# Rewriting an attention-plus-gate kernel as a stream of pair steps, with one PSUM rotation and the weights loaded behind batch 0

## The chip, the cores and the metric

The kernel runs on one core of one Trainium2 chip. The metric is device microseconds (us) of one execution, as the median of several runs. "PE" is TensorE, "DVE" VectorE, "ACT" ScalarE, "POOL" GpSimd. The granted clock is the share of full speed that the profile shows for PE; matmuls at full clock are called warm, those at half clock cold.

## The reference

Two stages follow each other for each of 8 batches (8 heads, 576 rows, 64 columns a head, 128 random features). The first is a random-feature attention; its output, laid out as 576 x 512, goes into a gated convolution that the kernel's authors and this text call "hyena".

```python
def phi(x):
    proj = np.einsum('bhsd,md->bhsm', x, omega)
    return np.concatenate([np.cos(proj), np.sin(proj)], axis=-1) / np.sqrt(m)
q_p, k_p = phi(q), phi(k)
kv  = np.einsum('bhsm,bhsd->bhmd', k_p, v);   z   = np.sum(k_p, axis=2)
num = np.einsum('bhsm,bhmd->bhsd', q_p, kv);  den = np.einsum('bhsm,bhm->bhs', q_p, z)
x = (num / den)                                # [...] guard of den, layout to (8, 576, 512)

proj = x @ w_proj;  x1, x2, x3 = proj[..., :D], proj[..., D:2*D], proj[..., 2*D:]
x2_conv = np.fft.irfft(np.fft.rfft(x2, axis=1) * np.fft.rfft(filter_fft, axis=0), axis=1)
out = (x1 * x2_conv * x3) @ w_out
```

## The kernel before

Heads go two at a time ("a pair"). A pair's features take a fixed path: a matmul with omega (`thk`, `thq`), DVE turns the phase into integer turns, POOL adds a quarter turn for the cosine (both write `angk`, `angq`), ACT takes the sine (`kf`, `qf`). `kv` and `nd` are the products with v and with q, `kvz` and `xsd` what DVE makes of them, `tx` a transpose into `xT`. In hyena, `eo` folds `xT` into even and odd halves, `x2p` projects it, `yp` and `ym` go to the spectrum, DVE multiplies by the filter (`tc`, `ymix`), POOL adds (`yg`), `xc` goes back, the gates (`x3p`, `x1p`) multiply, and `op` projects the output. The code is shortened.

```python
pt = tile_pool(name="pt", bufs=1, space=PSUM)     # phases, 2 banks
ph = tile_pool(name="ph", bufs=3, space=PSUM)     # attention
pm = tile_pool(name="pm", bufs=3, space=PSUM)     # filter and hyena
# [...] weights, filter and its spectrum first, then:
for b0 in range(B + 1):
    # [...] loads of q, k, v of batch b0; all v casts; all q transposes; tail features
    for hp in range(4):                           # attention of batch b0
        # k features of pair hp, q features of pair hp, each through _phases
        kvp = ph.tile([128, 2, 2, 1 + D], FP32, tag="ph")    # 40 matmuls on kf, kft
        nc.vector.tensor_scalar(kvz, kvp, 1.0 / KVS, None, ALU.mult)
        # nd, reciprocal, xsd ; the transpose of pair hp-1 stands between k and q features
    # then hyena of batch b0 - 1, all its PSUM tiles from pm
    eo = mo.tile([128, 4, 2, HS], FP16, tag="eo")
    # [...] x2p, yp, ym, four times (gates, inverse), op

def _phases(nc, pool, th, name):
    turns = pool.tile([128, 2, w], I32, tag="ang")
    nc.vector.tensor_scalar(turns[:, 0], th, TO_PHASE, None, ALU.mult)
    nc.gpsimd.tensor_scalar(turns[:, 1], turns[:, 0], 1.0, TURN / 4, ALU.mult, ALU.add)
    # [...] low 16 bits go to the sine
```

## Time and profile before

| | |
|---|---|
| time before the change | 531.08 us, 3 runs (530.04 to 532.85) |
| profiled span | 532.2 us |
| attention of batch 0, alone | about 50 us, at half clock |
| steady period (attention of b with hyena of b-1) | 54 to 58 us |
| hyena of the last batch, alone | 42 us |

Two rows of the page: the first is the granted TensorE clock in 40 equal slices of the span, in tenths (9 is 90% or more); the second shares out the chain of work that ended last, by engine.

```profile
PEclk9985565689998999999998999899999999999898
...
POOL 25%; DVE 19%; PE 18%; ACT 18%; issue 11%; DMA 6%; SPq 1%; POOLq 0%; DVEq 0%; ACTq 0%
```

The clock is low for long around batch 0's attention only. From 98.8 to 490 us, where the matmuls of both stages lie side by side, its mean is 0.98. No engine has more than a quarter of the chain: the steady stage is a relay from engine to engine, and PE has work of the other stage while it waits.

### The profile page before, as it was taken

The numbers are of one execution on the slowest core, as the hardware profiler recorded it, in microseconds if no ns is written. First come the engines' busy times: TensorE is split into PE (matmuls) and PEld (weight loads), VectorE is DVE, ScalarE is ACT, GpSimd is POOL, SyncE is SP. The second block draws the span as 40 slices with busy tenths as digits, with TensorE's granted clock in tenths as the row PEclk, the third lists the DMA queues.
The fourth block names the chain that finished last, engine by engine and source line by source line (L and its number), as shares of the span: only waits on it lengthen the run. The fifth ranks groups of instructions, "written<-read, shape, count | busy, mean of one in ns | idle before, by whom it ended". The sixth has DMA issues, their size and how long they took to land.

```text
span 532.2 us, 9767 instructions
## 1 busy us (share of the span) xinstructions
PE 390.3 (73%) x4042; PEld 250.4 (47%) x4042; DVE 307.1 (58%) x610; ACT 238.3 (45%) x316; POOL 249.7 (47%) x229
## 2 busy tenths in 40 slices
PE   0135456877897789768877888778967897778794
PEld 0012345445654555446535664456545654564371
DVE  1256435566754766567746684667567665763440
ACT  1012354245635463835563644466355635463222
POOL 3053943546446463655465456455246423442331
PEclk9985565689998999999998999899999999999898
DMA  8859943900366034901590058203400020002002
GB/s 247 232 122 144 108 33 40 139 1 1 46 174 51 1 41 127 102 1 12 119 140 2 1 103 153 16 1 46 164 10 1 3 80 10 1 2 77 14 0 89
DMA packets 71355, 35.30 MB, mean 66 GB/s; under 512 B 47760, under 2 KB 64656, under 8 KB 71312
## 3 DMA queue, kind: packets, MB, share of 16 engines
q0 software_dynamic: 51472, 11.56, 24.1%
q1 hardware_dynamic: 19840, 23.14, 13.4%
q8 instruction: 31, 0.51, 0.4%
q14 instruction: 12, 0.10, 0.1%
HBM read 36.80 MB, written 9.44 MB: 87 GB/s over the span
## 4 chain that ended last, share of the span: by engine, by line
POOL 25%; DVE 19%; PE 18%; ACT 18%; issue 11%; DMA 6%; SPq 1%; POOLq 0%; DVEq 0%; ACTq 0%
ACT qf L317 8%; POOL yT L415 6%; DVE angk L457 5%; POOL yg L383 5%; ACT kf L305 4%; DMA f<-in_moe_filter_fft_dram 4%; POOL angq L458 4%; DVE tc L380 4%; PE kv L331 3%; POOL qa L228 3%; POOL angk L458 3%; PE nd L341 3%; DVE xsd L350 3%; PE xc L94 2%; PE op L94 2%
## 5 line engine op out<-in xcount | busy, mean ns | idle before, releaser
L305 ACT ACTIVATE kf<-angk 128x2048 f16<-128x2048 int16 x32 | 61.1, 1908 | 48.6 <-POOL angk L458 48.6
L317 ACT ACTIVATE qf<-angq 128x2048 f16<-128x2048 int16 x32 | 61.1, 1911 | 21.3 <-POOL angq L458 21.3
L238 POOL TENSOR_TENSOR vl<-vf,vh 128x512 f16<-128x512 f32 x32 | 36.1, 1138 | 72.1 <-PE nd L341 43.1
L94 PEld LDWEIGHTS <-wph 128*128 128x128 f16 x512 | 48.7, 99 | 38.7 <-issue 24.7
L331 PEld LDWEIGHTS <-kf 128*128 128x128 f16 x1024 | 46.2, 105 | 43.5 <-ACT kf L305 43.5
L415 POOL TENSOR_TENSOR yT<-w,cv 128x576 f16<-128x576 f32 x32 | 45.4, 1417 | 40.1 <-DVE cv L414 35.5
L331 PE MATMUL kv<-vh,kf 128*128 128x65 f16 x512 | 40.7, 206 | 30.1 <-ACT kf L305 30.1
L458 POOL TENSOR_SCALAR angk<-angk 128x1024 int32<-128x1024 int32 x32 | 33.6, 1051 | 52.7 <-DVE angk L457 52.2
L397 ACT ACTIVATE x<-x3p 128x288 f32<-128x288 f32 x64 | 26.1, 409 | 69.6 <-PE x3p L94 68.6
L94 PE MATMUL x3p<-xT,wph 128*128 128x288 f16 x256 | 43.8, 290 | 15.8 <-DVE tc L380 11.8
L457 DVE TENSOR_SCALAR angq<-thq 128x1024 int32<-128x1024 f32 x32 | 39.1, 1222 | 19.3 <-ACT qf L282 11.5
L383 POOL TENSOR_TENSOR yg<-tc,tc 128x1024 f16<-128x1024 f32 x16 | 37.6, 2352 | 23.0 <-DVE tc L380 23.0
L228 POOL DMA_DIRECT2D qa<-in_q_dram x40 | 34.8, 887 | 22.4 <-PE tkt L259 13.1
L457 DVE TENSOR_SCALAR angk<-thk 128x1024 int32<-128x1024 f32 x32 | 39.1, 1221 | 10.4 <-PE thk L299 10.2
L94 PE MATMUL op<-wo,yT 128*128 128x512 f16 (+1 forms) x160 | 41.2, 380 | 4.8 <-POOL yT L415 4.1
L94 PE MATMUL x1p<-xT,wph 128*128 128x288 f16 x256 | 41.1, 290 | 3.9 <-DVE tc L380 1.8
L94 PE MATMUL x2p<-wph,eo 128*128 128x512 f16 x160 | 40.2, 386 | 3.2 <-ACT o L429 3.0
L429 ACT ACTIVATE o<-op 128x512 f32<-128x512 f32 (+1 forms) x40 | 23.0, 595 | 43.3 <-PE op L94 28.2
L94 PE MATMUL xc<-invh,yg 128*128 128x288 f16 x128 | 35.2, 289 | 8.7 <-DVE w L403 7.5
L458 POOL TENSOR_SCALAR angq<-angq 128x1024 int32<-128x1024 int32 x32 | 33.5, 1047 | 13.1 <-DVE angq L457 9.8
L341 PE MATMUL nd<-kvz,qf 128*128 128x65 f16 x640 | 27.5, 200 | 16.4 <-ACT qf L317 13.8
L331 PE MATMUL kv<-vl,kf 128*128 128x64 f16 x512 | 39.5, 204 | 0.0
(91 smaller groups left out, 822.4 us busy)
## 6 DMA issues: line engine op xcount, KB each, us to landing
vf<-in_v_dram SPq DMA_DIRECT2D x8, 1024.0 KB, 5.7
out_dram<-o SPq DMA_DIRECT2D x32, 256.0 KB, 2.2
ka<-in_k_dram POOLq DMA_DIRECT2D x8, 512.0 KB, 6.1
qa<-in_q_dram POOLq DMA_DIRECT2D x32, 128.0 KB, 4.2
f<-in_moe_filter_fft_dram SPq DMA_DIRECT2D x8, 256.0 KB, 12.5
wph<-in_moe_w_proj_dram POOLq DMA_DIRECT2D x4, 384.0 KB, 11.4
vft<-in_v_dram SPq DMA_DIRECT2D x16, 64.0 KB, 4.2
out_dram<-o SPq DMA_DIRECT2D x8, 128.0 KB, 2.7
```

The costliest lines, as they stand in the source:

```text
L94: nc.tensor.matmul(outap, l, r, start=(i == 0), stop=(i == n - 1))
L228: nc.gpsimd.dma_start(qall[: CH[c], c], q[b, :, 128 * c : 128 * c + CH[c], :].rearrange("h s d -> s h d"),)
L238: nc.gpsimd.tensor_tensor(vl[hp], vp, vh[hp][:, :, :, :D], ALU.subtract)
L305: nc.scalar.activation(kf.rearrange("p t a r m -> p t (a r m)"), ang, AF.Sin, scale=TO_ANGLE)
L317: nc.scalar.activation(qf[hp][:, :, :, :512].rearrange("p h t s -> p t h s"), ang.rearrange("p t (h s) -> p t h s", h=2), AF.Sin, scale=TO ...
L331: nc.tensor.matmul(kvp[:, hh, t, : 1 + D] if i < 5 else kvp[:, hh, t, :D], l, r_, start=(i == 0), stop=(i == len(terms) - 1),)
L341: nc.tensor.matmul(xps[:, c], qf[hp][:, hh, t, SOFF[c] : SOFF[c] + 128], kvz[:, hh, t], start=(t == 0), stop=(t == 1),)
L383: nc.gpsimd.tensor_tensor(yg[g], t[0], t[1], ALU.add)
L397: nc.scalar.mul(x3[:, ns], ps, YS / TIS)
L415: nc.gpsimd.tensor_tensor(yT[:, dc], w.rearrange("p a s -> p (a s)"), cv.rearrange("p a s -> p (a s)"), ALU.mult)
L457: nc.vector.tensor_scalar(turns[:, 0], th, TO_PHASE, None, ALU.mult)
L458: nc.gpsimd.tensor_scalar(turns[:, 1], turns[:, 0], 1.0, TURN / 4, ALU.mult, ALU.add)
```

## The change

The intent: features of the next pair are emitted ahead of this pair's products, so that PE need not wait for phase, quarter turn and sine of its own pair. The q features go in wider groups, some copies vanish, the weights and the filter are emitted behind the loads of batch 0, and all PSUM tiles but the phases share one rotation of six banks (one pool whose buffers are handed out in turn). It is a complete rewrite; this is its core.

```diff
-    pt = tile_pool(name="pt", bufs=1, PSUM)
-    ph = tile_pool(name="ph", bufs=3, PSUM)
-    pm = tile_pool(name="pm", bufs=3, PSUM)
+        self.pt = self.pool("pt", 1, space=psum)
+        self.ps = self.pool("ps", 6, space=psum)      # every tile has tag "ps"
 [...]
-    # weights, filter, spectrum; then per batch:
-    #   loads(b), v casts(b), q transposes(b), tails(b)
-    #   for hp: features(b, hp); products(b, hp)
-    #   hyena(b - 1)
+        self.omega_load()
+        self.loads(0)
+        self.buffers()
+        self.weights()                                # with the filter's spectrum
+        for b in range(B):
+            if b + 1 < B:
+                self.loads(b + 1)
+            if b == 0:
+                for hp in range(4):
+                    self.v_split(0, hp)
+                self.front(0, 0)
+            for hp in range(4):
+                if hp < 3:
+                    self.front(b, hp + 1)             # features of the next pair
+                elif b + 1 < B:
+                    self.front(b + 1, 0)
+                self.kv(b, hp)
+                if b + 1 < B:
+                    self.v_split(b + 1, hp)
+                self.attend(b, hp)
+                if hp:
+                    self.strip(b, hp - 1)
+            self.strip(b, 3)
+            if b:
+                self.hyena(b - 1)
+        self.hyena(B - 1)
 [...]
-            nc.scalar.mul(x3[:, ns], ps, YS / TIS)    # gates: x3, then w = x1p * x3
+                    nc.scalar.mul(w[:, ns], ps, YS / TIS)
+                    nc.vector.tensor_tensor(w[:, ns], ps, w[:, ns], ALU.mult)
-    t = mo.tile([128, 2, DM], FP32, tag=f"tc{i}")
+    t = mo.tile([128, 2, DM], FP32, tag=f"tc{i}", bufs=2)
```

## The prediction

> **What bounds the kernel now.** I read the page first (busy shares), then stretches of the run by stage, then the chain of work that ended last, then single engines in time.
>
> ```profile
> PE 390.3 (73%) x4042; PEld 250.4 (47%) x4042; DVE 307.1 (58%) x610; ACT 238.3 (45%) x316; POOL 249.7 (47%) x229
> ```
>
> No engine is full, so the answer lies in the stages. The columns of the next view are start:end, length, then busy us (instructions) of PE, PEld, DVE, ACT, POOL, then the granted clock, DMA share and GB/s.
>
> ```profile
> 0.00:24.81 24.81, 0.54 (x2) 0.34 (x3) 2.93 (x12) 1.80 (x3) 5.21 (x13) 1.00 0.95 257
> 48.60:98.80 50.20, 29.68 (x327) 22.16 (x327) 24.49 (x51) 19.71 (x17) 27.80 (x30) 0.53 0.71 87
> 213.00:270.00 57.00, 45.86 (x518) 29.65 (x518) 36.73 (x75) 29.96 (x40) 31.15 (x29) 1.00 0.41 68
> 490.00:532.20 42.20, 30.69 (x169) 17.42 (x168) 12.26 (x21) 11.82 (x25) 10.32 (x6) 0.87 0.13 44
> ```
>
> Four stages: a start in which only DMA works; batch 0, whose attention runs alone at half clock (50 us); seven steady periods of 54 to 58 us (mean 56, from 98.8 to 490) in which attention of batch b runs between the matmuls of the gate stage ("hyena") of batch b-1; and the last hyena alone (42 us). One attention alone plus one hyena alone is 50+42 = 92 us; together they take 56. That overlap is the kernel's main asset. The chain inside a steady period shows why it isn't shorter:
>
> ```profile
> 241.30 1.23 DVE angk L457
> 242.53 0.08 issue
> 242.60 1.04 POOL angk L458
> 243.65 1.38 POOL yT L415
> 245.02 1.02 POOL angq L458
> 246.04 0.02 issue
> 246.07 1.92 ACT qf L317
> 247.99 0.05 issue
> 248.03 0.50 PE nd L341 x10
> ```
>
> The start-to-start distance of a pair is 9.2 us (angk at 241.30, then at 250.46): DVE phase, POOL quarter turn, ACT sine, PE product, one after the other, with hyena work filling PE's gaps.
>
> **What the Trainium skill says.** (1) "TensorE: Matmul & The Clock Gate", Part 1: the default clock is half rate, a window of about 3.4 us decides, and its table of advice warns of idle gaps over about 3 us. The trace agrees on half rate but shows that less idling is enough. PE idled 2.44 us and the next matmuls ran at 0.50 for some 6 us:
>
> ```profile
> 501.49 1.12 PE L94 MATMUL x3p<-xT,wph 128*128 128x288 f16 x4 [2.44 <-DVE tc L380]
> 502.00:503.00 1.00, 0.60 (x3) 0.21 (x2) 1.00 (x2) 0.36 (x1) 0.36 (x1) 0.50 0.00 0
> 506.00:507.00 1.00, 1.00 (x6) 0.65 (x5) 0.46 (x1) 0.00 (x0) 0.00 (x0) 0.50 0.00 0
> ```
>
> (2) The same page, "Architectural detail": PE pulls weight loads ahead, but matmuls stay in program order, and ACT and DVE are strict FIFO. So the compiled order of each engine decides what can overlap. (3) "Trainium Kernel Development and Optimization", Key Constraints: DMAs of all queues run on the same 16 engines. The start agrees: both queues together filled them (share 0.95).
>
> **The change part by part.** I compared the compiled order of both kernels, engine by engine.
>
> *Lost overlap.* Before, PE's order alternates: kv of pair 1, xc, nd, x3p, x1p, kv of pair 2. After, in batches 2 to 7 it is all of the attention, then all of hyena (x2p, yp, ym, four times gates and inverse, op), then the next attention; DVE, ACT and POOL likewise. The separate three-bank PSUM pools became one rotation of six banks, handed out in emission order; I take that as the likely reason. So a steady period becomes A + H instead of about max(A, H).
>
> *H, from the rows of the lone hyena at the end of before.* There, x2p starts at 490.23 and op ends at 525.33: 35.1 us. The new kernel double-buffers tc and has six banks. tc costs 4 x 1.15 us start to start; the second yg (2.35) follows the fourth tc. With x2p 4.35, the first yp 0.65: 5.0+4.7+2.4 is about 12.3 us to the first inverse matmul, against 15.7 before. Then 1.5 for the first inverse, 3 x 3.63 for the other column blocks (before shows 3.6), 2.4 for od, cv and yT, 3.1 for op: 30.2 us. If the clock is low at its start, as I expect, about 2 us more: **H = 32**.
>
> *A, from the same rows.* DVE per batch: eight phases 9.2, two half phases 1.1, copies kT, qT, kTt 3.1, kvz 1.4, reciprocals and xsd 4.8, xT 1.5, v tails 1.6, eo 1.5: 24.2 us. That is the floor. POOL: 7 whole and 2 half turns and 4 vl (13.5) plus its DMA issues (0.89 x5, 0.64 x2, 0.95: 6.7) = 20 us. ACT: 8 sines of 1.91, two of 1.06, four casts of 0.61 = 19.8. PE 16. Walking the compiled orders from op's end: kf of pair 1 waits behind three qa issues (2.7 us) on POOL, so kv_1 at 6.6; kf_2 waits for qf_1_0, a cast and qf_1_1 on ACT, so kv_2 at 14.3; thk_3 stands inside kv_2 in PE's order, so kf_3 needs DVE, POOL and ACT after it: kv_3 at 19.4; its nd waits for the angle of the next batch's pair 0, 23.4; then rd, xsd, one more phase, two xT copies and eo (5.6 us of DVE) before x2p can start: 29.9. Looking one pair ahead is thus partly undone inside PE's fixed order. PE stands nearly still for 5 us at the end of A, enough by the 2.44 us case to lose the clock. With 1.5 us for slow matmuls: **A = 31.5**.
>
> *Start.* Batch 0's q, k and v now go first. But DVE's order has all five folds of the filter before kTt, ACT's order has ten filter copies before the first sine, so features still wait for the filter.
>
> ```profile
> q0 software_dynamic: 51472, 11.56, 24.1%
> q1 hardware_dynamic: 19840, 23.14, 13.4%
> ```
>
> The hardware queue moves 23.14 MB in 13.4% of 532 us (71 us): 325 GB/s. Up to the filter it now has v 1.18, fwd 0.98, filter 2.36 MB: 14 us. The software queue's q and k cost (128-11)/8 = 15 us a batch (11 us being the weights at the start, a share of 43.6% over 25 us), and share the engines. So the filter lands at about 30 us; kv_0 follows 9 us later (filter copies 5, table load 1.3, two sines 3): 38 us as the start of A0 on A's clock. A0 runs at half clock but without eo: 31 us.
>
> *Smaller.* Two-gate product in place, one xT copy fewer a pair, wider tail sines: 16 ACT and 38 DVE instructions fewer, under 1 us a batch.
>
> *Sum.* Start 38, A0 31, A1 31.5; hyenas 0 to 6, 7 x 32 = 224; A2 to A5 126; A6 without loads 29; A7 without a successor 24; the last hyena 29 as its head overlaps the one before; output 6: 538.5. Against before: start and batch 0, 98.8 becomes 69 (-30); end -8; seven periods of 56 become six of some 63 plus the first of 31.5 and one extra hyena in a row (+45).
>
> **The rivals.** (a) *The pipeline wins.* If the waits in A are shorter than I walked (A = 27, near DVE's 24.2) and the clock holds (H = 30), the seven A and seven H lose some 45 us: 495 to 505. For it: PE is busier per us than in batch 0 of before, and before's steady stage held a clock of 0.95 to 1.00. Against: the strict orders, POOL's DMA issues in front of angk, and 5 us of nearly idle PE at each seam. (b) *The clock falls in every A and stays low into H.* Batch 0 before shows 0.53 throughout. A = 34 and H = 34 make 560 to 570. Against: PE's hyena is dense, so recovery after 4 to 6 us is likely. (c) *DMA becomes the wait:* the single vf buffer is reloaded only after the last vl. A vf load takes 5.7 us to land and has a whole H to do it, so it is hidden; no change. (d) *The filter lands earlier or later* than 30 us: one for one, perhaps 5 us.
>
> **Range and chances.** A and H each have an error of about 2 us, common to six or seven repetitions, so 12 to 18 us; the start 5 to 7. I choose **538 us**, range 510 to 564. Faster by 2% means below 520.5, slower above 541.7. The centre is close to the upper border, and a rewrite with fewer instructions has upside I may have missed: faster 0.23, same 0.37, slower 0.40.
>
> **What would show each step.** The stretches of a steady period should show two alternating parts: one with PE near 16 busy us in about 31, DVE nearly full; one with PE near full for 30 to 33 and DVE, ACT, POOL each under half. PEclk should dip once a period, at the start of x2p. Summed DVE busy should drop little (about 10 us), PE's hardly. The first kv should start near 39 us, the second batch near 69. The first xc of a block should come 12 to 14 us after its x2p. I am wrong if hyena and attention overlap after all (a period under 58 us), if A is DVE-full without waits (about 26), or if the first kv starts before 33 us.

## The result, and the profile after

The changed kernel takes 557.59 us (4 runs, 555.85 to 562.23) against 531.97 us of the kernel before (4 runs in the same rounds, 530.04 to 534.3). The ratio is 1.0493, 95% interval 1.0412 to 1.0575: slower. A ratio here is the mean time of one kernel's fast runs over the mean of the other's fast runs of the same rounds, so it isn't quite the ratio of the medians. The profiled execution has a span of 560.4 us, and a mean granted clock of 0.85 against 0.919 before.

From the page of the changed kernel: busy time, clock by slice, and the chain by engine.

```profile
PE 413.3 (74%) x3994; PEld 275.1 (49%) x3994; DVE 309.0 (55%) x580; ACT 247.6 (44%) x300; POOL 252.4 (45%) x237
...
PEclk9865779888967897788968899778987789898998
...
PE 37%; POOL 21%; DVE 21%; DMA 7%; ACT 7%; issue 6%; POOLq 0%; DVEq 0%; ACTq 0%
```

PE executes 48 matmuls fewer and is busy 23 us longer, because the clock is now low in parts of every period. Its share of the chain has doubled.

The stages, cut at each start of `x2p` and each end of `op` (columns as in the prediction; the first stretch is cut at 44 us instead): the first four pairs and batch 1's attention, one attention and one hyena of the steady part, and the last hyena.

```profile
44.00:110.60 66.60, 43.73 (x645) 33.31 (x645) 50.39 (x94) 43.16 (x32) 45.21 (x49) 0.78 0.62 89
...
210.12:241.59 31.47, 21.38 (x329) 17.10 (x330) 24.36 (x46) 19.43 (x16) 20.48 (x22) 0.78 0.70 106
241.59:274.90 33.31, 29.68 (x171) 17.32 (x169) 13.77 (x24) 10.70 (x20) 10.50 (x7) 0.90 0.03 12
...
523.97:560.40 36.43, 26.59 (x169) 16.18 (x169) 11.98 (x21) 12.05 (x25) 10.28 (x6) 0.94 0.16 55
```

Attention (31.47 us) and hyena (33.31 us) stand one after the other; the place where they meet is called the seam below. In attention DVE has 24.36 us of 31.47, in hyena only 13.77; PE nearly fills hyena. One steady period is 64.8 us. The compiled order of PE shows why. Each word is a group of matmuls by tile, pair and count, around the first `x2p` of each kernel, first before, then after:

```
before: x2p_4x4 kv_0x40 yp_0_0x3 yp_0_1x3 nd_0_0x10 nd_0_1x10 tk_1x4 yp_1_0x3 yp_1_1x3 [...]
        x1p_0_0x4 x1p_0_1x4 kv_1x40 xc_0_0x6 xc_0_1x3 nd_1_0x10 nd_1_1x10 [...]
after:  kv_2x24 nd_2_0x10 nd_2_1x10 tx_1x5 tktx2 tk_0x4 tq_0x5 tq_1x5 kv_3x14 thtx4 kv_3x26 thk_0x4
        nd_3_0x10 nd_3_1x10 tx_2x5 thq_0_0x2 thq_0_1x2 tx_3x5 x2p_0x4 x2p_1x4 x2p_2x4 x2p_3x4 [...]
```

The head of one steady hyena in the chain that ended last (start us, us, what):

```profile
241.59 6.02 PE x2p L94 x20
...
249.06 2.28 DVE tc L432 x2
...
251.41 4.66 POOL yg L433 x2
...
256.11 3.06 PE xc L94 x12
```

Warm `x2p` takes 4.33 us and a warm `xc` group of 12 takes 1.47 us (the later groups of the same hyena do). Here the `xc` group is at half clock throughout and `x2p` for the most part. The waits of PE in front of such places (start, us, instruction, and in brackets the idle time before it and who ended it):

```profile
235.80 1.01 PE L342 MATMUL thq<-qT,om 128*128 128x512 f16 x2 [2.67 <-DVE angk L301]
...
256.11 0.42 PE L94 MATMUL xc<-invh,yg 128*128 128x288 f16 x1 [2.89 <-POOL yg L433]
```

And the start: DVE's part of the first tail phases (`angt`), POOL up to their quarter turn, and the first `kv` on PE:

```profile
28.82 0.69 DVE L301 TENSOR_SCALAR angt<-tht 128x512 int32<-128x512 f32 x1 [1.36 <-PE tht L311]
...
34.29 4.19 POOL L227 DMA_DIRECT2D qa<-in_q_dram  x5 [0.92 <-DMA wp<-in_moe_w_proj_dram]
38.55 4.37 POOL L290 TENSOR_TENSOR vl<-vf,vh 128x512 f16<-128x512 f32 x4
42.86 0.64 POOL L302 TENSOR_SCALAR angt<-angt 128x512 int32<-128x512 int32 x1
...
46.71 0.43 PE L372 MATMUL kv<-vh,kf 128*128 128x65 f16 x4
```

DVE had finished its part of `angt` at 29.5 us. POOL first issues five q loads of batch 1, then splits v, and gets to the quarter turn 13.4 us later. The first `kv` starts at 46.7 us.

Where the 22 us between the predicted 538.5 and the profiled 560.4 us lie:

| stage | predicted us | profiled us |
|---|---|---|
| start to the first `kv` | 38 | 46.7 |
| first `kv` to the first `x2p` (two attentions) | 62.5 | 63.9 |
| seven hyenas (0 to 6) | 224 | 233.9 |
| attention of batches 2 to 5 | 126 | 126.1 |
| attention of batches 6 and 7 | 53 | 53.3 |
| last hyena and output | 35 | 36.4 |

### The profile page after: what moved, and what is told of

It is laid out like the page before. It is cut to its first block, busy times and chain, and to the rows that moved or that the text cites. A ratio compares the mean times of both kernels' runs of the same rounds, so it can differ in the third digit from the quotient of the medians.

```text
span 560.4 us, 9625 instructions
## 1 busy us (share of the span) xinstructions
PE 413.3 (74%) x3994; PEld 275.1 (49%) x3994; DVE 309.0 (55%) x580; ACT 247.6 (44%) x300; POOL 252.4 (45%) x237
## 4 chain that ended last, share of the span: by engine, by line
PE 37%; POOL 21%; DVE 21%; DMA 7%; ACT 7%; issue 6%; POOLq 0%; DVEq 0%; ACTq 0%
PE xc L94 9%; PE x2p L94 8%; PE xg L94 7%; POOL yg L433 7%; ACT kf L329 4%; PE kv L372 4%; DVE angq L301 4%; POOL qa L227 4%; DVE tc L432 3%; PE op L94 3%; POOL yT L470 3%; POOL angk L302 3%; DMA qa<-in_q_dram 3%; DVE angk L301 3%; POOL vl L290 3%
## 5 line engine op out<-in xcount | busy, mean ns | idle before, releaser
L94 PE MATMUL xg<-xT,wp 128*128 128x288 f16 x512 | 69.2, 289 | 0.0
L94 PEld LDWEIGHTS <-wp 128*128 128x128 f16 x512 | 51.1, 100 | 15.6
L301 DVE TENSOR_SCALAR angq<-thq 128x1024 int32<-128x1024 f32 (+1 forms) x40 | 44.5, 1112 | 22.1 <-ACT kft L316 11.5
L342 PE MATMUL thq<-qT,om 128*128 128x512 f16 x64 | 23.3, 452 | 39.1 <-DVE angq L301 22.6
L302 POOL TENSOR_SCALAR angq<-angq 128x1024 int32<-128x1024 int32 (+1 forms) x40 | 40.2, 1006 | 25.5 <-DVE angq L301 24.4
L449 ACT ACTIVATE w<-xg 128x288 f32<-128x288 f32 x64 | 26.3, 411 | 56.3 <-PE xg L94 54.9
L94 PE MATMUL x2p<-wp,eo 128*128 128x512 f16 x160 | 47.9, 470 | 0.0
L468 DVE TENSOR_TENSOR cv<-xc,od 128x288 f32<-128x288 f32 x32 | 14.6, 458 | 58.3 <-PE xc L94 58.3
L466 ACT COPY od<-xc 128x288 f32<-128x288 f32 x32 | 12.8, 400 | 71.3 <-PE xc L94 71.3
L389 PEld LDWEIGHTS <-qf 128*128 128x128 f16 x640 | 31.2, 111 | 25.7 <-issue 19.7
```

Source lines behind the costliest of these rows:

```text
L94: nc.tensor.matmul(outap, l, r, start=(i == 0), stop=(i == n - 1))
L301: self.nc.vector.tensor_scalar(t[:, 0], th, TO_PHASE, None, ALU.mult)
L302: self.nc.gpsimd.tensor_scalar(t[:, 1], t[:, 0], 1.0, TURN / 4, ALU.mult, ALU.add)
L342: nc.tensor.matmul(th[:, 512 * i : 512 * (i + 1)], self.om2[:, hh], qT[:, 1024 * g + 512 * i : 1024 * g + 512 * (i + 1)], start=True, stop ...
L389: nc.tensor.matmul(ps[:, c], qf[:, t, hh, o : o + 128], kvz[:, hh, t], start=(t == 0), stop=(t == 1))
L449: nc.scalar.mul(w[:, ns], ps, YS / TIS)
```

## The experiments

The theory after the comparison had four parts. (1) One PSUM rotation in emission order makes attention and hyena serial, and this is the loss. (2) Looking one pair ahead is a gain, which the loss outweighs. (3) Hyena is longer than worked out because the clock falls at the seam, with `eo` as a second suspect. (4) The start is long because POOL's queue is in the way, not because of the filter. The rivals: that the new emission order itself (front of the next pair first) does the serializing; that lookahead is worthless; that `eo` and not the clock is the excess of hyena; and that the filter is what the features wait for. Ten kernels were run; all gave correct results. Kernels that differ from the changed kernel are compared with it by way of the kernel before, which ran in the same rounds.

### 1. The kernel before, with one rotation of six banks

```diff
-    ph = tile_pool(name="ph", bufs=3, PSUM)
-    pm = tile_pool(name="pm", bufs=3, PSUM)
+    ph = pm = tile_pool(name="ps", bufs=6, PSUM)     # and every tag "ph", "pm" becomes "ps"
```

> The kernel before with its two three-bank PSUM pools made one rotation of six, nothing else. Theory (the shared rotation in emission order takes the overlap of attention and hyena away): the compiled order is serial, a period becomes about 43 us of attention plus 32 of hyena, the whole 620 to 660 us. Rival (the overlap was lost for another reason, the rewrite's emission order, and six banks in one pool harm nothing): within 3% of 532.

Measured: 725.68 us, ratio 1.3628 (1.3534 to 1.3722). The direction was right, the size too small in my expectation. The clock row of its page:

```profile
PEclk9955555589766986578755796668955797559998
```

A period is 82 to 85 us. In the steady attentions the mean clock is 0.56 to 0.66, so that `kv` is slow as well. Nothing but the pools was changed, and the overlap is gone: with this emission order the rotation alone is enough to lose it. My explanation: a tile in a shared rotation waits for the tile handed out six before it, and with all of attention emitted ahead of all of hyena, hyena's first tile comes behind attention's last. The Trainium skill, "Perfetto Trace Analysis", section "Matmul Optimizations", asks to use all 8 PSUM banks for parallelism. Both kernels use all 8; what differs is which stages share a rotation, and this run shows 36% for it.

### 2. The changed kernel, with two rotations of three banks again

```diff
-        self.ps = self.pool("ps", 6, space=psum)
+        self.ps = self.pool("ps", 3, space=psum)
+        self.pg = self.pool("pg", 3, space=psum)     # hyena and the filter's spectrum take pg
```

> The changed kernel with the six-bank pool split into three for attention and three for hyena and filter. Theory (lost overlap costs the time): x2p, yp and ym move between the next pairs' products, the period falls from 64.7 to 52 to 58 us, the whole to 490 to 525 us. Rival (the clock and the chain inside attention cost the time, not the seams between the stages): the period stays above 62, the whole within 2% of 557.

Measured: 495.89 us, ratio 0.9324 (0.9276 to 0.9372): 7% faster than the kernel before, where the changed kernel is 5% slower. Its steady periods are 53 to 57 us. The compiled order of PE has both stages mixed again:

```
thk_1x4 kv_0x40 thq_1_0x2 x2p_0x4 x2p_1x2 thq_1_1x2 nd_0_0x10 nd_0_1x10 tk_2x4 x2p_1x2 x2p_2x4 x2p_3x1 kv_1x11 thk_2x4 kv_1x29 x2p_3x3 nd_1_0x10 [...]
```

Its page:

```profile
PE 382.1 (78%) x3994; PEld 249.9 (51%) x3994; DVE 312.5 (64%) x580; ACT 242.7 (49%) x300; POOL 253.7 (52%) x237
```

The same 3994 matmuls now take 382.1 us of PE, not 413.3, at a mean clock of 0.94. So the serial order costs the changed kernel twice, by waiting and by the clock. The emission order of the rewrite is unchanged here, so it doesn't serialize the stages by itself: the rival falls.

### 3. The changed kernel without the lookahead

```diff
-                if hp < 3:
-                    self.front(b, hp + 1)
-                elif b + 1 < B:
-                    self.front(b + 1, 0)
+                self.front(b, hp)                    # and no front(0, 0) ahead of the loop
```

> The changed kernel with each pair's features emitted in the pair's own step again, the rest as it is (serial stages, six banks in one rotation). Theory (looking one pair ahead shortens attention, the intended gain is real): attention grows from 31.5 to 42 to 52 us, as in the merged form of the kernel before; the hyena block stays at 33; the whole 640 to 720 us. Rival (PE's fixed order had undone the lookahead): attention stays under 36, the whole under 600.

Measured: 682.8 us, ratio 1.2804 (1.2748 to 1.286). The chain of this kernel, at the end of one hyena and the start of the next:

```profile
249.56 2.88 PE op L94 x12
...
301.04 4.33 PE x2p L94 x20
```

Attention lies between 252.4 and 301.0 us: 48.6 us, where the changed kernel needs 31.5. The lookahead is therefore worth some 17 us a batch in the serial form. (The mean clock of attention is lower as well, 0.65 against 0.78, so a part of this may be the clock.) The change contains a large gain and a larger loss.

### 4. The changed kernel with PE kept busy at the seam

```diff
+    def warm(self, name, n):
+        ps = self.bank([128, DM], name)
+        for _ in range(n):
+            self.nc.tensor.matmul(ps, self.ident, self.wp[0][:, :DM], start=True, stop=True)
 [...]  # 4 and 5 of them at the end of attention, 9 ahead of the first inverse; nothing reads them
```

> The changed kernel with matmuls that nothing reads put into PE's idle stretches: 4 and 5 at the seam before hyena, 9 ahead of the first inverse of each hyena. Clock theory: x2p falls from 6.0 to about 4.4 us and the first inverse pair from 3.06 to about 1.5, so 3 us in each of 8 hyenas, 20 to 25 us in all (532 to 540). Rival (the low clock lies beside other waits and costs nothing): within 1% of 557, or slower by the matmuls added.

Measured: 542.22 us, ratio 1.0175 (1.0126 to 1.0224), a little above what was expected. 144 matmuls that nobody reads make the kernel faster by (1.0493 - 1.0175) x 532 = 17 us. From the chain of one hyena of it:

```profile
233.37 4.33 PE x2p L94 x20
...
246.22 1.65 PE xc L94 x12
```

`x2p` is at 4.33 us in every hyena, and the first `xc` group takes 1.65 us instead of 3.06. The low clock in hyena is a cost of its own, and it comes from the thin PE work at the seam. This isn't offered as a cure; experiment 2 fills the same gaps with useful work.

### 5. The changed kernel with batch 1's loads, the weights and the filter behind batch 0's first pairs

```diff
         self.buffers()
-        self.weights()
 [...]  # in the pair loop of batch 0:
+                    if hp == 0:
+                        self.loads(1)
+                    elif hp == 1:
+                        self.weights()
+                    elif hp == 3:
+                        for i in range(4):
+                            self.v_split(1, i)
```

> The changed kernel with batch 1's loads issued after pair 0 of batch 0 and the weights after pair 1. Theory (POOL, stuck in its own queue behind the issues of weights and of batch 1's loads until 42.9 us, holds the first features): the first kv comes at 25 to 31 us and not at 46.7, the first hyena at 92 to 100 and not at 110.6, the whole 10 to 18 us shorter. Rival (the filter or q's landing at 26.7 us holds it): the first kv stays after 38 us, the gain is under 6 us.

Measured: 541.01 us, ratio 1.0144 (1.0089 to 1.0198). One of the four runs, at 547.43 us, counts as slow; the ratio is from the other three (538.4 to 541.55). POOL now gets to the quarter turn at 12.67 us and the first `kv` starts at 29.46:

```profile
12.67 0.61 POOL L302 TENSOR_SCALAR angt<-angt 128x512 int32<-128x512 int32 x1 [4.33 <-DVE angt L301]
...
29.46 0.42 PE L372 MATMUL kv<-vh,kf 128*128 128x65 f16 x4
```

The first `x2p` moves from 110.59 to 94.95 us; the next three periods stay at 64.7 to 65.4 us. A start that does the two things at once doesn't tell POOL's queue from the filter, so the next run moves one of them.

### 6. The changed kernel with only batch 1's loads moved

```diff
-            if b + 1 < B:
-                self.loads(b + 1)
             if b == 0:
                 for hp in range(4):
                     self.v_split(0, hp)
                 self.front(0, 0)
+            if b + 1 < B:
+                self.loads(b + 1)
```

> The changed kernel with one move: batch 1's q, k and v loads are issued after batch 0's v casts and the features of its first pair, not before them; the weights stay where they are. Theory (POOL's queue held up the start): POOL is then free for the first vl and the quarter turn once the wo issues are out, at some 27 us, so the first kv moves from 46.7 us to 34 to 36, all later stages shift by 8 to 12 us, and the ratio to the kernel before is 1.025 to 1.034 (1.049 for the changed kernel). Rival (the weights and the filter ahead of the features held it up, as my prediction said): the first kv stays above 43 us and the ratio above 1.042.

Measured: ratio 1.0153 (1.0101 to 1.0204), same or slower unclear, from the two fast runs, 540.2 us each. Two more runs took 551.3 and 556.2 us and count as slow, being over 1.5% above the fastest of this kernel; all four have a median of 545.77. In the profiled run the quarter turn follows directly on v:

```profile
27.30 4.35 POOL L290 TENSOR_TENSOR vl<-vf,vh 128x512 f16<-128x512 f32 x4
31.63 0.61 POOL L302 TENSOR_SCALAR angt<-angt 128x512 int32<-128x512 int32 x1
...
37.51 0.40 PE L372 MATMUL kv<-vh,kf 128*128 128x65 f16 x4 [1.62 <-ACT kf L329]
```

The first `kv` starts at 37.5 us and the first `x2p` at 101.27, 9.3 us earlier than in the changed kernel. That is the shift expected of POOL's queue (the first `kv` itself was expected at 34 to 36), and the rival, above 43 us, falls. Experiment 5 goes 8.0 us further, from 37.5 to 29.46: that much belongs to the weights and the filter ahead of the features, so both are causes, of nearly equal size.

The profiled run is 22 us shorter than the changed kernel's, though only 9.3 us come from the start. The rest is in hyenas 0 to 3, of which the first is partly and the others are fully warm here, without a line of them changed. So the totals of experiments 5 and 6, which agree, don't compare their starts; the first `kv` does. No trace was kept of the two slow runs, so whether they are slow by cold hyenas stays open. One of the warm hyenas, in the chain:

```profile
226.00 4.33 PE x2p L94 x20
...
238.84 1.64 PE xc L94 x12
```

From the start of `x2p` to the end of `op` it takes 30.1 us; the same code in the changed kernel takes 33.31. Of the 3.2 us, 1.69 are `x2p`, 1.42 the first `xc`. And the wait of PE ahead of that `xc` is the same:

```profile
238.84 0.30 PE L94 MATMUL xc<-invh,yg 128*128 128x288 f16 x1 [2.89 <-POOL yg L433]
```

After 2.89 us of idling the matmul takes 0.30 us here and 0.42 in the changed kernel. So the length of a gap alone does not decide about the clock; the next run shows it within one kernel.

### 7. The changed kernel with two buffers for eo

```diff
-        eo = mo.tile([128, 4, 2, HS], FP16, name=f"eo{b}", tag="eo")
+        eo = mo.tile([128, 4, 2, HS], FP16, name=f"eo{b}", tag="eo", bufs=2)
```

> The changed kernel with two buffers for eo instead of one; the order of every engine is the same. Theory (eo stands in DVE's order ahead of tc and waits for x2p's end): eo runs while x2p runs, tc starts 0.8 to 1.3 us earlier against the end of x2p, hyena is some 1 us shorter, in sum 5 to 9 us, ratio 1.033 to 1.040. Rival (the whole excess of hyena over 32 us is the clock): no change, ratio 1.046 to 1.052.

Measured: 545.46 us (545.3 to 546.13), ratio 1.025 (1.021 to 1.029). That is more than either theory allowed, 13 us less than the changed kernel, so the expectation missed. The trace divides it. A warm hyena takes 29.4 us here and 30.1 in experiment 6, so `eo` is worth 0.7 us a hyena, 5 us in all: the right sign, and a little under the 0.8 to 1.3 us that I gave it. The rest is clock again: of the seven hyenas, three are fully warm (29.4 us), others not (33.5 us at worst). Here are two seams of this one run, with the same instructions in the same order, in steps of 1 us:

```profile
171.00:172.00 1.00, 0.00 (x0) 0.00 (x0) 1.00 (x2) 0.95 (x1) 0.02 (x1) 1.00 0.26 60
...
173.00:174.00 1.00, 1.00 (x6) 0.49 (x5) 0.96 (x2) 0.78 (x1) 0.19 (x1) 1.00 0.00 0
...
232.00:233.00 1.00, 0.00 (x0) 0.00 (x0) 1.00 (x2) 0.71 (x1) 0.26 (x1) 0.50 0.11 25
...
235.00:236.00 1.00, 1.00 (x4) 0.33 (x3) 1.00 (x2) 1.00 (x1) 0.00 (x0) 0.50 0.00 0
```

In both PE idles for one whole slice shortly ahead of `x2p`. The first `x2p` runs at full clock, 6 matmuls a slice, the second at half, 4 a slice. Read in steps of 0.1 us, the granted clock of this stretch goes down at 153.8, up at 160.6, down at 167.5, up at 170.9, down at 215.3, up at 222.1, down at 228.9 and up at 239.1. The low stretches are 6.8, 3.4, 6.8 and 10.2 us: multiples of 3.4. The Trainium skill, "TensorE: Matmul & The Clock Gate", Part 1, says that the window of activity is 3413 ns long and free-running, so that it depends on the phase where a change lands. The trace agrees with a grid of 3.4 us.

For the gap ahead of the first `xc` the clock records of the kept traces can be sorted by it. In the changed kernel and experiments 3, 5 and 6, 28 hyenas have the same 2.89 or 2.90 us of idle PE there. In 13 of them the first `xc` matmul takes 0.30 us and starts 0.96 to 1.84 us after the last grid edge. In 15 it takes 0.42 us and starts 0.06 to 0.82 us after an edge, once 0.01 us before one. So the place on the grid separates warm from cold there without exception, though no run sets it on purpose. For the seam ahead of `x2p` it doesn't: the two shown above start 1.93 and 1.94 us after an edge. PE was busy for 3.12 us of the 3.41 us before that edge in the first and for 2.73 us in the second; what decides there stays open.

### 8. Two rotations and the early start together

Experiments 2 and 5 in one kernel.

> Split PSUM pools and the earlier start of batch 0 together. If the two causes are independent, the gains add: 496 less about 14 gives 478 to 486 us. Rival (the start's gain is taken back later, since the weights come later and the first hyena now starts among attention): 490 or more.

Measured: 487.68 us, ratio 0.9154 (0.9114 to 0.9194). That lies between the theory and the rival. By the ratios the start gave (0.9324 - 0.9154) x 532 = 9 us on top of experiment 2, where 14 were expected and experiment 5 gained (1.0493 - 1.0144) x 532 = 19 over the changed kernel. The traces show why. The first `kv` of experiment 2 and then of this run:

```profile
42.75 0.43 PE L376 MATMUL kv<-vh,kf 128*128 128x65 f16 x4
...
32.42 0.43 PE L376 MATMUL kv<-vh,kf 128*128 128x65 f16 x4
```

Here the early start moves it by 10.3 us, and in experiment 5 by 17.3 (46.71 to 29.46). Experiment 5 also had hyenas that turned warm in later batches.

### 9. Hyena emitted in pieces within the pair steps

On top of experiment 8, with two buffers for `eo` (the diff is shortened; which piece stands where is in the comments):

```diff
                 self.kv(b, hp)
 [...]
+                if b: self.piece(b - 1, hp, 0)    # x2 / gates 0 / gates 1 / inverse 2
                 self.attend(b, hp)
 [...]
+                if b: self.piece(b - 1, hp, 1)    # after strip: spectrum / inverse 0 / inverse 1, gates 2 / gates 3, inverse 3
             self.strip(b, 3)
             if b:
-                self.hyena(b - 1)
+                self.project_out(b - 1)
```

> The changed kernel with split pools, the earlier start, two eo buffers, and hyena of the batch before emitted in pieces within the four pair steps. Theory (the order of emission decides the overlap): all of hyena stands between products of attention, the period falls to 46 to 51 us (PE has some 41 to 45 us of work in it), the whole to 440 to 470 us. Rival (split pools alone have got the overlap already, and more mixing only adds waits on the strict queues): within 2% of the run with split pools and the earlier start.

Measured: 466.82 us (466.7 to 467.17), ratio 0.8755 (0.873 to 0.878). It is the fastest kernel and beats both. Against experiment 8 it gains 4%, so the rival falls; how much of that the second `eo` buffer gives was not tried alone. The steady period is 53.2 to 53.7 us; the total lies in the expected range, the expected period was missed by some 2 us. Its page:

```profile
PE 370.0 (80%) x3994; PEld 249.1 (54%) x3994; DVE 318.8 (69%) x580; ACT 239.0 (51%) x300; POOL 253.5 (55%) x237
...
PEclk9999869999999999998999999999999999999998
```

### 10. The same with one rotation of six

```diff
-        self.ps = self.pool("ps", 3, space=psum)
-        self.pg = self.pool("pg", 3, space=psum)
+        self.ps = self.pool("ps", 6, space=psum)
```

> As the run before it, but with the six banks in one rotation as in the changed kernel. Theory (one rotation loses overlap only because banks are handed out in emission order, so it is harmless where the emission is mixed): within 2% of the run before it. Rival (one rotation is bad in itself, as a bank held by one stage stops the other): over 5% slower than it.

Measured: 471.07 us, ratio 0.8835 (0.8809 to 0.8861), within 1% of experiment 9. One rotation costs 36% (kernel before, experiment 1) or 13% (changed kernel over experiment 2) where the stages are emitted one after the other, and 1% where they are emitted mixed. The harm lies in rotation and emission order together.

## Why the prediction was right or wrong

**The verdict and the range** held: slower was given the highest chance, by a small margin, and 557.6 us lies in 510 to 564. The centre was 20 us too low, and by itself it lay below the border of slower (541.7 us); that the verdict came true was partly luck.

**Lost overlap: right.** The period is A + H. That the single rotation is the reason was marked as likely in the prediction; experiments 1 and 2 show it from both sides, and experiment 10 that it takes the emission order as well.

**A = 31.5: right in sum, with wrong terms.** Measured 31.47; the hit is luck. `eo` isn't on the way at the end of attention: `x2p` follows `tx` directly, and DVE does the next batch's `eo` later, behind `x2p`. In its place the chain runs through the casts and differences of the v tails on DVE (`vth`, `vtl`: 2.7 us of it), which the walk had only in DVE's sum. The walk itself was close up to `kv` of pair 3 (7.3, 15.0 and 20.9 us where it said 6.6, 14.3 and 19.4); the `nd` behind it came 26.5 us after `op`, not 23.4. The clock is 0.78 to 0.80 on average in the attentions of batches 2 to 6, not low at their end only. That this costs 1.5 us isn't shown: in experiment 6 two attentions with a mean clock of 0.78 and 0.84 take 31.47 and 31.48 us.

**H = 32: the step that failed by size is the clock term.** The prediction had 30.2 us of warm work and 2 us for a low clock. Warm hyenas of the same code take 30.1 us (experiment 6), so the warm sum was right (12.8 us to the first `xc`, where it said 12.3). A cold one costs 3.2 us more, not 2, because the clock falls twice, at `x2p` and again before the first `xc`. The six cold ones and the half-warm last one make 233.9 us instead of 224. `eo` in front of `tc`, which I had suspected afterwards, is 0.7 us of the warm sum.

**Start = 38 us: the step that failed by mechanism.** It read: "the filter lands at about 30 us; kv_0 follows 9 us later". The last fold of the filter was done on DVE at 21.3 us, so by that sum `kv` would have started near 30. It started at 46.7, because POOL, whose queue I had not walked through in this stage, stood in DMA issues that wait for earlier DMAs until 38.5 us, then in four v splits. Moving batch 1's loads away from there brings the first `kv` forward by 9.2 us; moving weights and filter too, by a further 8.0 (experiments 6 and 5). An error of one sign and one of the other met, and 8.7 us were left.

**The smaller claims.** "PEclk should dip once a period" is wrong: it dips in attention and twice in hyena. "Summed DVE busy should drop little (about 10 us)" is wrong: it went from 307.1 to 309.0 us. "PE's hardly" is wrong: it rose by 23 us, by the clock (the same matmuls take 382.1 us in experiment 2, against 390.3 in the kernel before). In attention PE was to have "near 16 busy us" and DVE to be "nearly full": they have 21.4 and 24.4 of 31.47. The second batch was due near 69 us; its first `kv` starts at 80.7. The first `xc` was to come 12 to 14 us after `x2p`: it comes after 12.8 us warm and 14.5 cold. Three slips of the working changed little: 5.0+4.7+2.4 is 12.1, not 12.3; POOL has eight whole quarter turns a batch, not seven (it is busy for 20.5 us, where the text has 20); and the "+45" of the cross-check is 42.5 by the terms of the sum. For the order of matmuls it names "Architectural detail"; that half of its sentence stands in Part 2 of the same page, and no run here tests it.

**The rivals.** Rival (b), the clock low in every attention and into hyena, at 560 to 570 us, is nearest to what happened; I gave it too little. What spoke against it, "recovery after 4 to 6 us is likely", was about right for each dip in hyena (back at full clock 4.0 us after the start of `x2p`, 3.1 us after the first `xc`) but forgot that there would be a second one. Rival (a), the pipeline wins, happened neither in A nor in H; but its 495 to 505 us is about what the same rewrite reaches with two rotations, by an overlap that the rival didn't claim. Rival (c), the v load, stayed hidden, and rival (d) went the other way, as told above.

## What to carry to other kernels

A PSUM pool is also a statement of order: stages that should overlap either get rotations of their own or are emitted mixed, piece by piece, and the compiled order of PE tells whether they do. Read the start of a kernel on every engine's own queue, the DMA-issuing one first, since a quarter turn of 0.6 us waited 13 us here, mostly behind loads that nobody needed yet. When matmuls come in two speeds from one period to the next with the same instructions, look at the granted clock before inventing a wait.

## What the Trainium skill lacked or had wrong

- "TensorE: Matmul & The Clock Gate", the table in "Why this matters for your kernels", warns of PE-idle gaps over about 3 us. Gaps under that were enough here: the clock fell around gaps of 2.67 and 2.89 us, and after 2.44 us in the kernel before. But a gap of 2.89 us in experiment 6 left it at full rate. A limit by length alone doesn't tell the two apart; the place of the gap on the grid of 3.4 us did (experiment 7).
- "Perfetto Trace Analysis", "Matmul Optimizations", asks for all 8 PSUM banks and doesn't say that a rotation shared by two stages orders them. It made the kernel before 36% slower.
- No page that I found says that DMA issues on POOL can hold up the compute instructions behind them for long. Here POOL's queue was held by them until 38.5 us, while work that DVE had made ready at 29.5 us waited.
